# A pinned issue order, a channel mixer in two coupled streams, loads in order of use, and work moved to POOL, in an attention and mixer kernel

## Chip, cores, metric

One core of one Trainium2 chip. The metric is the device time of one execution in microseconds (us); the median of several runs is given. Slow runs are left out of all comparisons. PE is the matrix engine, DVE the vector engine, ACT the scalar engine, POOL the general engine that also issues most loads here.

## The reference, cut

Four batches, eight heads of 768 tokens and 64 columns: attention with a block mask, then a mixer over tokens and one over channels with a hidden width of 2048.

```python
def _attn_ref(q, k, v, sampled_blocks):
    scores = scale * np.matmul(q, k.transpose(0, 1, 3, 2))
    mask = ...                       # neighbours, first and last block, 3 sampled blocks per row
    scores = np.where(mask, scores, -1000000000.0)
    attn = softmax(scores)           # written out with max, exp and sum
    return np.matmul(attn, v)

def _moe_ref(x, alpha1, beta1, w_tok, alpha2, beta2, w_ch1, w_ch2, lam):
    a1 = alpha1 * x + beta1
    tok = np.einsum('ts,bsd->btd', w_tok, a1)
    u = x + lam * tok
    a2 = alpha2 * u + beta2
    ch = np.maximum(a2 @ w_ch1, 0.0) @ w_ch2
    return u + lam * ch
```

## The kernel before

The work is cut into 144 units (4 batches x 4 pairs of heads x 9 units of 1024 score columns). A unit is one set of score products (PE), one exponential (ACT) and, two units later, eight value products (PE). After nine units a pair of heads is normalised (DVE) and goes through the token mixer (`pair_mix`). After four pairs a batch can enter the channel mixer, whose products fill PE beside the next batch's attention. Parts, with cuts marked:

```python
    # weights: each in one piece, issued by POOL ahead of or beside the pairs' loads
    nc.gpsimd.dma_start(w1b[:], moe_w_ch1.rearrange("(o p) n -> p o n", p=P))
    ...
    def prepare(b, n):                       # a pair's casts, transposes and copies
        for i, src in enumerate((q2, k2)):
            nc.vector.tensor_copy(out=rel[...], in_=src[...])
        ...                                  # transposes on PE; q and k copied by DVE
        nc.vector.tensor_copy(out=vx[...], in_=v2[...])      # L220, the value copy

    def pair_mix(b, n):
        nc.vector.tensor_tensor(out=a1p[:], in0=x_sb[...], in1=bc(a1_bc, NT), op=ALU.mult)   # L298
        nc.vector.tensor_tensor(out=a1p[:], in0=a1p[:], in1=bc(b1_bc, NT), op=ALU.add)       # L301
        for g in range(2):                   # 18 token products on PE each
            ...
            nc.vector.tensor_tensor(out=sl, in0=sl, in1=tp[:], op=ALU.add)                   # reads PSUM
            nc.vector.tensor_tensor(out=ub[...], in0=sl, in1=bc(a2_bc, 3), op=ALU.mult)
        ...

    def ch_mix(b):                           # first product, then second: one after the other
        for hf in range(2):
            for f in range(16): ...          # 4 products, relu on ACT or DVE
            for m in range(3):  ...          # 16 products into one bank, added to x_sb, stored

    def setup_ch():
        nc.vector.tensor_copy(out=lam_bcb[:], in_=lam_bc[:])
        nc.vector.tensor_copy(out=be2b[:], in_=be2T[:])
        ...
        for g in range(8):                   # lam is folded into the second weight
            nc.vector.tensor_mul(out=w2b[...], in0=w2b[...], in1=lam_bcb[...])               # L407
```

The softmax here doesn't subtract the row's maximum and nothing guards it: scores larger than these inputs give would overflow.

## Time and profile before

Median 393.35 us (392.55 to 393.9). The profiled run spans 389.8 us.

| stretch of the profiled run before | us |
|---|---|
| start to first score product | 16.6 |
| from there to the first mixer product (in it 11.6 in which nothing computes) | 71.9 |
| from there to PE's last product | 297.4 |
| from there to the end | 3.9 |

The table is read from the timeline of PE: a stretch ends where a named product starts. The shares, the table of stretches and the waits behind it are in the prediction below.

### The profile page before, as it was taken

How to read it: one execution, taken by the hardware profiler on the slowest of the kernel's cores; microseconds unless marked ns; L12 is line 12 of the kernel's file. 1: busy time of each engine (PE TensorE's matmuls, PEld its weight loads, DVE VectorE, ACT ScalarE, POOL GpSimd, SP SyncE). 2: the span in 40 equal slices, each digit the busy share in tenths (PEclk: the TensorE clock that was granted, in tenths of full speed). 3: DMA queues.
4: the chain of work that ended last, by engine and by line, in shares of the span. 5: the costliest groups of instructions: out<-in, count | busy, mean ns of one | idle time of the engine just before them, and what ended most of it. 6: DMA issues, size and time to landing. Idle time of an engine off the chain costs nothing.

```text
span 389.8 us, 7791 instructions
## 1 busy us (share of the span) xinstructions
PE 343.3 (88%) x3398; PEld 219.8 (56%) x3398; DVE 210.3 (54%) x412; ACT 190.2 (49%) x209; POOL 35.9 (9%) x53
## 2 busy tenths in 40 slices
PE   0498089999999999999999999999999999699995
PEld 0276067775655656566656656576656665454442
DVE  3674089776564657374744756565537553632331
ACT  1167066786626655375626654566445564130220
POOL 7152012221011010101000000000000000000000
PEclk9999669999999999999999999999999999999999
DMA  8999994442204132323101000100010001000102
GB/s 190 240 211 205 206 158 64 63 62 27 36 29 102 15 42 49 67 49 42 23 29 54 2 2 29 55 2 2 2 54 29 3 0 56 29 0 27 56 0 81
DMA packets 20781, 23.26 MB, mean 60 GB/s; under 512 B 2068, under 2 KB 16524, under 8 KB 20620
## 3 DMA queue, kind: packets, MB, share of 16 engines
q0 software_dynamic: 15248, 14.42, 23.8%
q1 hardware_dynamic: 5192, 7.96, 5.9%
q8 instruction: 26, 0.43, 0.4%
q10 hardware_dynamic: 308, 0.40, 0.3%
q14 instruction: 7, 0.06, 0.0%
HBM read 30.90 MB, written 6.29 MB: 95 GB/s over the span
## 4 chain that ended last, share of the span: by engine, by line
PE 65%; DVE 12%; DMA 9%; ACT 9%; issue 3%; POOL 1%; ACTq 0%; DVEq 0%; POOLq 0%
PE mm L338 20%; PE mm L363 20%; PE sps L236 10%; ACT eT L245 8%; DMA w2b<-in_moe_w_ch_dram 7%; PE mm L310 6%; PE ops L259 5%; DMA v_103<-in_v_dram 2%; PE mm L213 2%; DVE hts L350 2%; DVE x_sb L318 2%; DVE a1p L298 1%; DVE a1p L301 1%; DVE ub L319 1%; ACT hts L346 1%
## 5 line engine op out<-in xcount | busy, mean ns | idle before, releaser
L245 ACT ACTIVATE eT<-sps,expb 128x1024 f16<-128x1024 f32 x144 | 154.2, 1115 | 115.4 <-PE sps L236 114.5
L338 PE MATMUL mm<-uT,w1b 128*128 128x384 bf16 x512 | 97.5, 325 | 2.8 <-DVE uT L326 0.6
L363 PE MATMUL mm<-w2b,hts 128*128 128x512 bf16 x384 | 91.3, 379 | 0.1
L346 ACT ACTIVATE hts<-mm,b1t 128x384 bf16<-128x384 f32 x64 | 37.1, 580 | 67.7 <-PE mm L338 67.4
L338 PEld LDWEIGHTS <-w1b 128*128 128x128 bf16 x512 | 47.8, 97 | 38.6 <-issue 8.6
L259 PEld LDWEIGHTS <-eT 128*128 128x128 f16 x1152 | 57.8, 99 | 19.7 <-issue 0.6
L350 DVE TENSOR_SCALAR hts<-mm,b1t 128x384 bf16<-128x384 f32 x64 | 39.5, 617 | 49.1 <-PE mm L338 48.9
L363 PEld LDWEIGHTS <-hts 128*128 128x128 bf16 x384 | 34.9, 97 | 35.1 <-issue 0.6
L373 DVE TENSOR_TENSOR ot<-x_sb,mm 128x512 f32<-128x512 f32 x24 | 16.5, 686 | 56.3 <-PE mm L363 56.2
L310 PE MATMUL mm<-a1p,wtokT 128*128 128x128 bf16 x576 | 35.4, 219 | 3.2 <-DVE a1p L301 2.9
L310 PEld LDWEIGHTS <-wtokT 128*128 128x128 bf16 x576 | 33.6, 98 | 5.3 <-issue 4.1
L318 DVE TENSOR_TENSOR x_sb<-x_sb,mm 128x384 f32<-128x384 f32 x32 | 17.6, 551 | 23.1 <-PE mm L310 23.1
L236 PE MATMUL sps<-qx_74,kx_78 88*128 88x512 bf16 (+1 forms) x96 | 24.0, 349 | 5.3 <-ACT eT L245 4.2
L236 PE MATMUL sps<-qx_76,kx_80 88*128 88x512 bf16 (+1 forms) x96 | 22.8, 325 | 3.5 <-ACT eT L245 3.5
L236 PE MATMUL sps<-qx_75,kx_79 88*128 88x512 bf16 (+1 forms) x96 | 25.1, 325 | 0.8 <-ACT eT L245 0.8
L236 PE MATMUL sps<-qx_77,kx_81 88*128 88x512 bf16 (+1 forms) x96 | 25.1, 339 | 0.5 <-ACT eT L245 0.5
L259 PE MATMUL ops<-vext_146,eT 128*128 128x65 f16 x432 | 23.9, 195 | 0.0
L325 PE MATMUL mm<-identb,ub 128*128 128x128 bf16 x96 | 10.0, 225 | 12.5 <-DVE x_sb L318 12.1
L213 PE MATMUL mm<-identb,rel 128*128 128x128 bf16 x192 | 17.1, 230 | 4.0 <-DVE qx_74 L184 4.0
L259 PE MATMUL ops<-vext_147,eT 128*128 128x65 f16 x360 | 20.5, 196 | 0.0
L259 PE MATMUL ops<-vext_148,eT 128*128 128x65 f16 x360 | 19.8, 193 | 0.0
L213 PEld LDWEIGHTS <-rel 128*128 128x128 bf16 x192 | 14.2, 103 | 8.6 <-issue 5.4
(146 smaller groups left out, 239.5 us busy)
## 6 DMA issues: line engine op xcount, KB each, us to landing
out_dram<-ot SPq DMA_DIRECT2D x24, 256.0 KB, 2.0
w1b<-in_moe_w_ch_dram POOLq DMA_DIRECT2D x1, 2048.0 KB, 22.4
w2b<-in_moe_w_ch_dram POOLq DMA_DIRECT2D x1, 2048.0 KB, 26.0
wtk<-in_moe_w_tok_dram POOLq DMA_DIRECT2D x1, 1152.0 KB, 15.0
a_bc<-in_moe_alpha_dram SPq DMA_DIRECT2D x2, 256.0 KB, 11.1
q2f<-in_q_dram SPq DMA_DIRECT2D x1, 384.0 KB, 3.1
k2f<-in_k_dram ACTq DMA_DIRECT2D x1, 384.0 KB, 4.0
lam_bc<-in_moe_lam_dram SPq DMA_DIRECT2D x1, 256.0 KB, 6.7
```

Source lines behind the costliest of these rows:

```text
L213: nc.tensor.transpose(tps[:, o, :], rel[:, a, o, :], identb[:])
L236: nc.tensor.matmul(sps[:, f - u * UN : f - u * UN + w], kx[h][0:KC, ts(jt, P)], qx[h][0:KC, c : c + w], start=True, stop=True,)
L245: nc.scalar.activation(eT[:], sps[:], AF.Exp, bias=expb[:], scale=SCALE)
L259: nc.tensor.matmul(ops[(b, n, a)][:, t, 0 : D + 1], eT[:, ts(i, P)], vx[:, a, jt, 0 : D + 1], start=(r == 0), stop=(jt == NT - 1), skip_gr ...
L310: nc.tensor.matmul(tp[:, j, :], wtokT[:, s, ts(3 * g + j, P)], a1p[:, s, :], start=(s == 0), stop=(s == NT - 1),)
L318: nc.vector.tensor_tensor(out=sl, in0=sl, in1=tp[:], op=ALU.add)
L325: nc.tensor.transpose(up[:, t, :], ub[:, t, :], identb[:])
L338: nc.tensor.matmul(hp[:], w1b[:, dk, ts(f, P)], uT[:, dk, ts(hf, HS)], start=(dk == 0), stop=(dk == 3),)
L346: nc.scalar.activation(hts[:, f, :], hp[:], AF.Relu, bias=b1t[:, f : f + 1], scale=1.0)
L350: nc.vector.tensor_scalar(out=hts[:, f, :], in0=hp[:], scalar1=b1t[:, f : f + 1], scalar2=0.0, op0=ALU.add, op1=ALU.max,)
L363: nc.tensor.matmul(cp[:], hts[:, nk, ts(m, P)], w2b[:, nk, :], start=(nk == 0), stop=(nk == 15),)
L373: nc.vector.tensor_tensor(out=ot[:], in0=x_sb[:, b % NXB * NT + t, :], in1=cp[:], op=ALU.add)
```

## The change

The intent: PE was at 315 us of work in 390, and the rest was to be closed up. The order of instructions on every engine is pinned to the program's, instead of being left to the scheduler. The mask comes first and the first pair is loaded in halves. Loads are issued in the order of use, and the weights in pieces. The channel mixer becomes two streams, so that a group of the first product and a chunk of the second alternate. Scaling the second weight (`w2b`) and the value copies move from DVE to POOL. In batch 0 the token sums come in single tiles. The tail of the last mixer uses the banks that attention has left. The diff, cut to its core:

```diff
+def pin_order(nc, tc):
+    last = {}
+    for ins in list(nc.cur_bb.bb.instructions):
+        prev = last.get(ins.engine)
+        if prev is not None:
+            tc.add_manual_dep(ins, prev, ..., reason="program order")
+        last[ins.engine] = ins.name
...
-        nc.vector.tensor_copy(
+    def put_v(b, n, v2, eng=nc.gpsimd):
+        eng.tensor_copy(out=vx[:, :, :, 0:D], ...)
...
+        m = 1 if b == 0 and n < NPAIR - 1 else 3       # tiles per token group
...
+    def scale_w2(g):
+        if g == 0:
+            nc.gpsimd.tensor_copy(out=lam_bcb[:], in_=lam_bc[:])
+        nc.gpsimd.tensor_tensor(
+            out=w2b[:, 2 * g : 2 * g + 2, :], in0=w2b[:, 2 * g : 2 * g + 2, :],
+            in1=lam_bcb[:].unsqueeze(1).broadcast_to([P, 2, DM]), op=ALU.mult)
...
+    def ch_next(tail=False):
+        ...                                            # what of either product can run
+        if can1 and can2:
+            two = (g2 - 12 * k2) * 16 < f * 12 if k1 == k2 + 1 else True
...
+            if i in (10, 12, 14, 16):                  # w1b in four pieces
+            if i in (20, 22, 24, 26):                  # w2b in four pieces
+            if i == NS:
+                mix_add(None, setup_ch(), i)           # NS = 36: be2b cast, 64 one-column products
+            if NS - 4 <= i < NS + 4:
+                scale_w2(i - NS + 4)                   # units 32 to 39
...
+    while mixq or st["g1"] < NF1 or st["g2"] < NF2:
+        mix_next(i)
+        ch_next(True)                                  # the tail, four banks for the first product
+        i += 1
+    pin_order(nc, tc)
```

## The prediction

> **What bounds the kernel now.** I read the page's busy shares first, then the slices, then busy time by stretches that I cut at the places where the slices change, then the timeline at the cuts. The page:
>
> ```profile
> PE 343.3 (88%) x3398; PEld 219.8 (56%) x3398; DVE 210.3 (54%) x412; ACT 190.2 (49%) x209; POOL 35.9 (9%) x53
> PE   0498089999999999999999999999999999699995
> PEclk9999669999999999999999999999999999999999
> ```
>
> PE is the bound in the middle, but not at the start (first two slices, and a hole at slice 5 with the clock down after it) nor near the end (a dent at slice 35). Busy by stretch:
>
> ```profile
> 0.00:16.60 16.60, 2.27 (x15) 1.41 (x16) 6.86 (x26) 1.28 (x1) 9.02 (x16) 1.00 0.95 216
> 16.60:38.40 21.80, 20.02 (x235) 14.81 (x236) 14.07 (x30) 15.44 (x15) 7.08 (x10) 1.00 1.18 209
> 38.40:50.00 11.60, 0.00 (x0) 0.00 (x0) 1.20 (x3) 0.43 (x1) 1.94 (x3) 0.63 1.25 205
> 50.00:80.00 30.00, 27.89 (x418) 21.69 (x418) 25.93 (x54) 21.75 (x21) 5.72 (x9) 0.91 0.58 84
> 80.00:88.50 8.50, 7.79 (x116) 5.90 (x112) 5.88 (x12) 6.63 (x8) 1.47 (x3) 1.00 0.52 71
> 88.50:334.00 245.50, 238.11 (x2355) 152.01 (x2356) 137.19 (x260) 135.33 (x150) 10.72 (x15) 1.00 0.15 32
> 334.00:341.00 7.00, 3.45 (x45) 2.64 (x45) 5.13 (x9) 0.00 (x0) 0.00 (x0) 1.00 0.11 40
> 341.00:385.90 44.90, 43.80 (x221) 21.38 (x220) 13.43 (x23) 9.30 (x16) 0.00 (x0) 1.00 0.08 30
> 385.90:389.80 3.90, 0.00 (x0) 0.00 (x0) 0.64 (x1) 0.00 (x0) 0.00 (x0) 0.98 0.18 67
> ```
>
> Columns after the length: PE, PEld, DVE, ACT, POOL, clock, DMA share, GB/s. The first score product starts at 16.58; the channel mixer (L338, L363) starts only at 88.5; between 38.4 and 50.0 nothing computes. The timeline names the causes:
>
> ```profile
> 7.02 0.36 DVE L220 COPY vext_146<-v_97 128x768 f16<-128x768 f16 x1 [4.03 <-DMA v_97<-in_v_dram]
> ...
> 13.06 0.36 DVE L220 COPY vext_147<-v_103 128x768 f16<-128x768 f16 x1 [2.24 <-DMA v_103<-in_v_dram]
> ...
> 48.80 0.69 DVE L407 TENSOR_TENSOR w2b<-w2b,lam_bcb 128x1024 bf16<-128x1024 bf16 x1 [11.77 <-DMA w2b<-in_moe_w_ch_dram]
> ...
> 336.65 2.17 PE L310 MATMUL mm<-a1p,wtokT 128*128 128x128 bf16 x36 [2.88 <-DVE a1p L301]
> ```
>
> Three times DVE, which works in order, sat at an instruction whose load had not come while ready work stood behind it (4.0, 2.2 and 11.8 us); at the end PE waits for the last pair's DVE chain with nothing to fill.
>
> "Busy" does not give PE's rate, so I take starts:
>
> ```profile
> 162.74 0.60 PE L236 MATMUL sps<-qx_77,kx_81 88*128 88x256 bf16 x3
> 163.17 0.41 PE L259 MATMUL ops<-vext_147,eT 128*128 128x65 f16 x8
> 163.42 1.02 PE L363 MATMUL mm<-w2b,hts 128*128 128x512 bf16 x4
> 164.28 0.60 PE L236 MATMUL sps<-qx_74,kx_78 88*128 88x512 bf16 x3
> ...
> 189.86 2.17 PE L310 MATMUL mm<-a1p,wtokT 128*128 128x128 bf16 x36
> 191.87 0.81 PE L338 MATMUL mm<-uT,w1b 128*128 128x384 bf16 x4
> 192.52 0.38 PE L236 MATMUL sps<-qx_77,kx_81 88*128 88x512 bf16 x1
> ```
>
> A score unit costs 0.43 us start to start, eight value products 0.24, four second products 0.86, 36 token products 2.01, four first products 0.65; six transposes 0.34 (same stretch). Times the counts: 144 units x 0.67 = 96.5; 16 pairs x (2.01 + 3 x 0.34) = 48.5; first products 128 x 0.65 = 83.2 to 83.5; second 96 x 0.86 = 82.9; weight setup 36 transposes (2.0) and 64 one-column products (1.7). **PE's work is 315 us of the 389.8.** The other 75 us: 16.6 before the first score product; 28.4 up to 88.5 (71.9 long, in which 45 units with their share of the rest need 43.5); 18 in 88.5 to 334 (245.5 for 227.5); 4.7 at the last pair; 3.1 in the last mixer; 3.9 after the last product.
>
> **The Trainium skill.** "Perfetto Trace Analysis", Identifying the Most-Contended Engine: matmul busy share is no measure of headroom, since matmuls are pipelined. The trace agrees: 343.3 busy, 315 of work. "TensorE: Matmul & The Clock Gate", Part 1: after about one idle window (3.4 us) the array falls to half rate, and about as much work brings it back; a 512-column product takes 216 ns at full rate. The trace agrees: clock 0.63 in the hole, eight value products 0.64 us at 50.7 against 0.41 later; 48 second products in 10.37 us. "GPSIMD Engine Reference", 4.1 and 8: two-input elementwise work is about twice as slow there as on DVE, and the engine shares SBUF interfaces with DVE. The kernel before has no such work on POOL, so its trace shows nothing of it.
>
> **The change, part by part.**
>
> *Start.* The mask comes before anything that waits for values, and q and k of the first pair arrive in halves. The table is in by 2.81 (first DVE compare); six compares and maxima and one scale, spaced about 0.2, end near 4.2 instead of 9.2. The full q load took 3.1 us from 1.22, the k load 4.0 from 1.37; halves should be in by 4.5, cast by 5.0. The identity load took 5.0 us from 1.68; it may set the transposes at about 6. Six transposes cold (0.85), a q copy (0.55), the mask copy of 768 columns from PSUM (about 0.9, twice L184's columns): first score product near 8.4. Gain 8.2. The eight warm-up products end near 4.7 and help little.
>
> *Hole.* Scaling w2b (8 x 0.68 us) and the value copies (16 x 0.36) go to POOL; the weights are loaded in pieces at units 10 to 26, after what attention needs. Loads up to unit 36 are some 10 MB, about 50 us at the 205 to 216 GB/s seen, so no faster than wanted, but in order of use. Hole gone: 11.6, and about 2 of cold clock.
>
> *First stage.* I stepped the new loop's counters through by arithmetic (order only, no times). The mixer can't start before batch 0 is mixed: unit 57. Until then a unit's PE work averages 57.5/57 = 1.01 us. ACT needs 1.02 (seven exponentials in 7.14 at 28.70). DVE, per batch 0 pair of nine units: two casts 0.70, four copies 2.2, two normalisations 1.5, a1p 1.9, uT 0.55, and the token sums, now in single tiles, 12 x 0.28 = 3.4 (L318's 0.551 less 256 elements at 0.96 per ns, an estimate): 10.25, or 1.14 a unit. Three engines nearly level, DVE first. I give 17 units at 1.1, 40 at 1.14 and 4 for coupling: **68 us**, 10.5 over PE's work.
>
> *The rest.* From unit 57 on 315 - 57.5 = 257 of PE work. Each unit gets one or two groups of first product and chunks of second, 2.19 us of PE against 1.02 + 0.29 of ACT; the second product has a bank of its own, so an eviction (0.58, 0.62) hides behind it. Of the 7.3% lost in 88.5 to 334 I leave 3%: **265 us**. By the count 44 groups and 45 chunks are left after the last unit, of which some belong to batch 2 and fill the last pair's DVE chain (4.7 gained); with four banks for the first product its 190 ns a piece in the last mixer (1.52 for eight) returns to 163 (3.1 gained).
>
> *End.* Unchanged, 3.9 to 4.1.
>
> Sum: 8.4 + 68 + 265 + 4.1 = 345.5 of span. The median before lies 3.5 above the profiled span; so 349.
>
> **Rivals.**
> 1. *DVE takes the first stage.* With POOL now computing (w2b scaling perhaps 1.4 us each, twice 0.68, by the skill) and sharing with DVE, and one value bank per head from batch 1 on, 1.14 becomes 1.4 a unit, as in 50 to 80 before (21 units in 30 us). For it: DVE 25.93 of 30 there. Against: that stretch held the w2b scaling and cold clock, which go. Time: +12, 361.
> 2. *A fixed order blocks.* If a load is late, or POOL, with value copies behind w2b's wait, is late, everything behind stands, as at 37 to 49 before. For it: POOL issues every later load from the same queue. Against: each load is asked for ten or more units ahead. Time: +5 to +12.
> 3. *The order is better than I grant*: 1% lost after unit 57 and 1.06 a unit before. For it: the interleave leaves no two groups on the same bank within an eviction. Time: 8 + 62 + 260 + 4 = 334, so 338.
> 4. *The gain is given back:* PE-bound anyway, only the start counts. Against: 75 us are not PE work.
>
> **Range and chances.** The fixed parts (315, end 4) are sure to 2; the start to 2; the first stage 62 to 80; the loss after it 1 to 5% (2.6 to 13). Together 340 to 362. Slower or same would need all 40 us of gain lost, with start and hole (20) seen plainly: 0.97 faster, 0.02 same, 0.01 slower.
>
> **What would show it.** First score product at 8 to 9; no DVE wait for w2b and PE clock full from about 10 on; 57 units by 76; DVE over 90% busy in 20 to 70; first L338 near 76 instead of 88.5; PE starts within 3% of work after that; no PE wait for a1p at the last pair; L338 at 163 ns in the last stretch. A hole behind a POOL instruction, or units at 1.4, would make me wrong upwards; DVE well under 90% in the first stage, downwards.

## The result, and the profile after

The changed kernel took 369.48 us (364.88 to 370.0, four runs). The kernel before took 392.95 in the same session (392.08 to 393.9). The ratio is 0.938 (95% interval 0.931 to 0.945). Ratios in this document are the mean time of one kernel's fast runs over that of the other's fast runs of the same rounds, so they are not quite the ratio of the medians. The direction was right, the size was not: 23.5 us gained of 44 expected, 7.5 us above the top of the range.

The profiled run is the fastest of the four (364.88 us, span 363.1). The others span 367 to 368, and what follows is read from the fast one alone.

The page of the changed kernel, busy shares and slices (compare the page of before in the prediction):

```profile
PE 329.7 (91%) x3372; PEld 216.6 (60%) x3406; DVE 219.3 (60%) x413; ACT 191.9 (53%) x212; POOL 77.5 (21%) x95
...
DVE  4479999579856756484666557474646553233221
...
POOL 6876599812300202030300000000000000000000
PEclk9699995599999999999999999999999999999999
```

POOL's busy time has doubled from 35.9 us. The clock is down in slice 2, near the start, and in slices 7 and 8, which is 54 to 73 us, where before it was down in slices 5 and 6. There is still a hole. Busy time by stretches, cut at unit 0, the hole's two ends, the first mixer product and PE's last product (length, then PE, PEld, DVE, ACT, POOL, clock, DMA share, GB/s):

```profile
8.70:51.10 42.40, 39.30 (x554) 30.02 (x554) 34.36 (x79) 38.36 (x38) 31.26 (x42) 0.92 1.15 206
51.10:68.80 17.70, 1.62 (x29) 1.12 (x25) 16.12 (x8) 1.10 (x2) 17.68 (x14) 0.58 0.63 93
68.80:96.50 27.70, 25.29 (x416) 20.60 (x414) 21.87 (x52) 20.59 (x20) 6.67 (x9) 0.96 0.44 61
96.50:359.50 263.00, 257.97 (x2370) 162.76 (x2400) 142.12 (x260) 129.15 (x151) 16.49 (x22) 1.00 0.15 35
359.50:363.10 3.60, 0.00 (x0) 0.00 (x0) 0.62 (x1) 0.00 (x0) 0.00 (x0) 1.00 0.19 73
```

In the hole PE worked for 1.62 of 17.7 us. DVE was "busy" for 16.12 us there with eight instructions, so they averaged 2 us each; those eight are the ones to look at. The timeline of DVE in the hole, where the numbers are start and duration:

```profile
51.13 1.89 DVE L359 TENSOR_TENSOR ub<-x_sb,a_bc 128x128 bf16<-128x128 f32 x1
52.95 0.18 DVE L311 RECIPROCAL rcp<-cp 128x6 f32<-128x6 f32 x1
53.16 0.56 DVE L314 TENSOR_TENSOR x_sb<-cp,rcp 128x384 f32<-128x384 f32 x1
53.64 2.17 DVE L336 TENSOR_TENSOR a1p<-x_sb,a_bc 128x768 bf16<-128x768 f32 x1
55.85 11.23 DVE L339 TENSOR_TENSOR a1p<-a1p,b_bc 128x768 bf16<-128x768 bf16 x1
67.00 0.16 DVE L445 CAST be2b<-be2T 128x4 bf16<-128x4 f32 x1
```

The same addition (L339) took 0.957 us in nearly every other pair. Here it took 11.23. POOL at the same time:

```profile
46.41 8.59 POOL L463 TENSOR_TENSOR w2b<-w2b,lam_bcb 128x1024 bf16<-128x1024 bf16 x4 [0.68 <-DMA w2b<-in_moe_w_ch_dram]
...
57.16 6.26 POOL L463 TENSOR_TENSOR w2b<-w2b,lam_bcb 128x1024 bf16<-128x1024 bf16 x3
63.37 0.81 POOL L261 COPY vext_77<-v_552 128x768 f16<-128x768 f16 x1
64.16 2.11 POOL L463 TENSOR_TENSOR w2b<-w2b,lam_bcb 128x1024 bf16<-128x1024 bf16 x1
```

The last multiplication ends at 66.27 (64.16 + 2.11), and the held addition ends at 67.08, which is 0.81 later: about its own normal duration. The shorter holds fit as well. The row of four from 46.41 ends its third multiplication at 52.85 (three quarters of 8.59), and `ub` ends at 53.02; the fourth ends at 55.00, and the first `a1p` instruction ends at 55.81. The two instructions between, L311 and L314, read PSUM and took their normal 0.18 and 0.56 beside the same multiplications. And PE waited for the cast that stood behind the held addition, in its own timeline:

```profile
67.31 0.56 PE L450 MATMUL mm<-be2b,w1b 128*128 128x1 bf16 x16 [16.08 <-DVE be2b L445]
```

With order pinned, all that PE had to do for the next units stood behind these 16 small products.

The rest of the changed kernel went as predicted: the first score product at 8.03 (predicted 8.4, before 16.58); 263.0 us from the first mixer product to PE's last product (predicted 265); 3.6 to the end (predicted 4.1). At the last pair PE waits 1.39 us for DVE where it waited 2.88:

```profile
290.67 1.17 PE L349 MATMUL mm<-a1p,wtokT 128*128 128x128 bf16 x18 [1.39 <-DVE a1p L339]
```

| stretch | predicted | after, profiled run |
|---|---|---|
| start to first score product | 8.4 | 8.03 |
| from there to the first mixer product, at unit 57 | 68 | 88.4 |
| from there to PE's last product | 265 | 263.0 |
| to the end | 4.1 | 3.6 |
| span | 345.5 | 363.1 |

So the miss lies in one row of the sum. Within it, units 0 to 37, counted from the start of one exponential to that of the other, took 42.4 us, 1.146 each (predicted 1.14); then came the hole; then units 38 to 57 took 27.7 us, 1.46 each (predicted 1.14 too).

### The profile page after: what moved, and what is told of

Read it like the earlier page. It is cut to its first block, busy times and chain, and to the rows that moved or that the text cites. A ratio compares the mean times of both kernels' runs of the same rounds, so it can differ in the third digit from the quotient of the medians.

```text
span 363.1 us, 7834 instructions
## 1 busy us (share of the span) xinstructions
PE 329.7 (91%) x3372; PEld 216.6 (60%) x3406; DVE 219.3 (60%) x413; ACT 191.9 (53%) x212; POOL 77.5 (21%) x95
## 4 chain that ended last, share of the span: by engine, by line
PE 74%; DVE 15%; DMA 5%; POOL 2%; issue 2%; SPq 0%; ACT 0%; ACTq 0%
PE cp L416 18%; PE mm L384 18%; PE sps L276 12%; PE mm L349 8%; PE ops L297 7%; DVE a1p L339 4%; PE ops L416 4%; PE sps L384 4%; PE mm L218 2%; DMA v_165<-in_v_dram 2%; DVE a1p L336 2%; DMA q_339<-in_q_dram 2%; DVE x_sb L314 2%; PE mm L365 1%; DVE ub L359 1%
## 5 line engine op out<-in xcount | busy, mean ns | idle before, releaser
L384 PE MATMUL mm<-uT,w1b 128*128 128x384 bf16 x424 | 85.1, 325 | 0.9 <-ACT hts L392 0.9
L416 PE MATMUL cp<-w2b,hts 128*128 128x512 bf16 x288 | 76.3, 379 | 2.0
L396 DVE TENSOR_SCALAR hts<-mm,b1t 128x384 bf16<-128x384 f32 x42 | 25.9, 616 | 43.1 <-PE mm L384 43.0
L358 DVE TENSOR_TENSOR x_sb<-x_sb,mm 128x384 f32<-128x384 f32 (+1 forms) x44 | 19.5, 443 | 18.8 <-PE mm L349 18.1
L396 DVE TENSOR_SCALAR hts<-sps,b1t 128x384 bf16<-128x384 f32 x22 | 13.6, 617 | 28.2 <-PE sps L384 28.2
L339 DVE TENSOR_TENSOR a1p<-a1p,b_bc 128x768 bf16<-128x768 bf16 x16 | 25.6, 1600 | 0.6
L276 PE MATMUL sps<-qx_67,kx_71 88*128 88x512 bf16 (+1 forms) x96 | 24.4, 355 | 1.4 <-DVE qx_67 L234 1.0
L425 DVE TENSOR_TENSOR ot<-x_sb,cp 128x512 f32<-128x512 f32 x20 | 13.7, 686 | 18.4 <-PE cp L416 18.3
L276 PE MATMUL sps<-qx_68,kx_72 88*128 88x512 bf16 (+1 forms) x96 | 22.9, 333 | 0.0
L359 DVE TENSOR_TENSOR ub<-x_sb,a_bc 128x384 bf16<-128x384 f32 (+1 forms) x44 | 21.9, 498 | 1.5
L276 PE MATMUL sps<-qx_70,kx_74 88*128 88x512 bf16 (+1 forms) x96 | 22.1, 325 | 0.1
L276 PE MATMUL sps<-qx_69,kx_73 88*128 88x512 bf16 (+1 forms) x96 | 22.2, 325 | 0.0
L297 PE MATMUL ops<-vext_75,eT 128*128 128x65 f16 x360 | 19.0, 197 | 0.6 <-DVE x_sb L314 0.6
## 6 DMA issues: line engine op xcount, KB each, us to landing
w1b<-in_moe_w_ch_dram POOLq DMA_DIRECT2D x4, 512.0 KB, 10.1
```

What stands on the lines that cost most here:

```text
L276: nc.tensor.matmul(sps[:, f - u * UN : f - u * UN + w], kx[h][0:KC, ts(jt, P)], qx[h][0:KC, c : c + w], start=True, stop=True,)
L297: nc.tensor.matmul(ops[(b, n, a)][:, t * VW : t * VW + D + 1], eTs[(b, n, u)][:, ts(c, P)], vx[:, a, jt, 0 : D + 1], start=(r == 0), stop= ...
L359: nc.vector.tensor_tensor(out=ub[:, gs, :], in0=sl, in1=bc(a2_bc, m), op=ALU.mult)
L384: nc.tensor.matmul(hp[:, 0:HS], w1b[:, dk, ts(f, P)], uTs[b][:, dk, ts(hf, HS)], start=(dk == 0), stop=(dk == 3),)
L396: nc.vector.tensor_scalar(out=hts[k][:, f, :], in0=hp[:, 0:HS], scalar1=b1t[:, f : f + 1], scalar2=0.0, op0=ALU.add, op1=ALU.max,)
L416: nc.tensor.matmul(cps[k][:], hts[k][:, nk, ts(m, P)], w2b[:, nk, :], start=(nk == 0), stop=(nk == 15),)
```

## The experiments

The first theory: POOL's multiplications of `w2b` hold DVE instructions, and the pinned order hands the hold on to PE. The rivals: w2b's load or product is late; pinning itself blocks; DVE is simply full. In all that follows, "changed" is the changed kernel at 369.48. The medians of the kernel before lay between 391.74 and 392.95 over the sessions of these runs, and each ratio is to that kernel on the same chip.

### Taking the multiplications away from POOL

**e1_no_scale.** Nothing is scaled; the result is wrong.

```diff
-            if NS - 4 <= i < NS + 4:
-                scale_w2(i - NS + 4)
```

> The changed kernel without the eight multiplications of w2b on POOL (wrong result on purpose). Theory A: while POOL runs them (46.4 to 66.2 us), DVE instructions with two SBUF inputs cannot finish (one a1p add took 11.23 us instead of 0.96), and PE starves for 16.6 us. Then the hole and the cold clock after it go: span 363 - 16.6 - 2 = 344 to 347, median 346 to 350, no DVE a1p or ub over 1.2 us. Rival B: a load or a value copy behind the fixed order of POOL is what is late, the long add only shows it; then part of the hole stays with another wait ahead of it, span over 353. Rival C: the first stage is DVE-bound by volume: units 38 to 57 stay at 1.4 us or more, span about 350.

Measured: 353.27 us (352.31 to 355.63), ratio 0.902. The hole shrinks to one PE wait of 3.35 us for the `be2b` cast. About 16 of the 20 us missed hang on eight POOL multiplications and one cast of `lam`. No `a1p` or `ub` took more than 0.96, as theory A said, but its time was missed by 3 us: units 38 to 57 still took 1.46 each and the span is 350.9, which is what rival C had said. So the hole is the multiplications' doing, and the slow units after it are not.

**e2_dve_same.** The same work at the same places, on DVE.

```diff
-            nc.gpsimd.tensor_copy(out=lam_bcb[:], in_=lam_bc[:])
-        nc.gpsimd.tensor_tensor(
+            nc.vector.tensor_copy(out=lam_bcb[:], in_=lam_bc[:])
+        nc.vector.tensor_tensor(
```

> The same eight multiplications at the same places of the order, on DVE instead of POOL. Theory A: no hole of 16 us; DVE gets 8 x 0.68 = 5.4 us more in a stage where it is nearly full, and may wait up to 4 us in order for the w2b pieces (they landed at 46.4 to about 53.7 in the changed kernel, the multiplications stand at units 32 to 39, 44 to 52 us): span 350 to 356, median 352 to 359. Rival B: nothing gained, span 360 or more, since the late load is still waited for. Rival C: volume on DVE is the bound, so moving more to it costs at least 5 us over the run without the multiplications and the units after 38 stay slow.

Measured: 358.79 us (358.29 to 360.83), ratio 0.916. Moving the multiplications back to the engine that was thought too full for them gains 10.7 us. They took 0.68 us each on DVE, and 2.12 on POOL in the changed kernel: the change saved 5.5 us of DVE time here and lost some 16 for it (e1). Rival B is out: at these places DVE did not wait for w2b's load at all, and POOL had waited 0.68 us for it in the changed kernel. One wait of PE remains, 5.62 us before the small products of `be2b` (see e7).

**e3_dve_late.** On DVE, at units 57 to 64, just before the second product needs the weight.

```diff
-            if NS - 4 <= i < NS + 4:
-                scale_w2(i - NS + 4)
+            if 57 <= i < 65:
+                scale_w2(i - 57)
```

> The multiplications on DVE at units 57 to 64, where PE is the bound and DVE has slack, just before w2b is first used (unit 66). Theory A: within 3 us of the run without them, span 345 to 350, median 347 to 352, right result, the best version so far. Rival C: the first stage is as slow as in that run. If DVE is late there after all, evictions of the first product wait for it and it costs up to 5 us more.

Measured: 353.9 us as the median of the fast runs, ratio 0.902. One run of 358.45, the profiled one, counted as slow and is left out. After unit 57 DVE has room, so the multiplications cost next to nothing there: the time is that of the run without them (353.27). The range of theory A (347 to 352) was missed by 2 us.

**e4_pool_spread.** On POOL, but spread: one multiplication for every third unit, from unit 40 to 61.

```diff
-            if NS - 4 <= i < NS + 4:
-                scale_w2(i - NS + 4)
+            if 40 <= i < 64 and i % 3 == 1:
+                scale_w2((i - 40) // 3)
```

> The multiplications stay on POOL but one in every third unit from 40 to 61 instead of eight in a row from 32 to 39. Theory A: each holds a two-input DVE instruction for at most its own 2.1 us, and not every one meets such an instruction, so the hole breaks into pieces: 8 x up to 2.1, half of them met, 6 to 12 us instead of 16.6; span 351 to 360. If the holding is by the row of them without a gap, less: 347 to 352. Rival B (lateness, not sharing): no long DVE instruction and no hole at all, as in the run without them.

Measured: 370.65 us (370.55 to 370.72), ratio 0.945. Spreading them in the program did not help, and all the times expected were missed. POOL still ran them close together (59.00 to 66.04 without a gap), and this time the held instruction is tiny, a cast of four columns with one input, in the timeline of DVE of this run:

```profile
57.59 8.49 DVE L445 CAST be2b<-be2T 128x4 bf16<-128x4 f32 x1
```

It normally takes 0.16 us, and it ends at 66.08 as POOL's row does. So a hold isn't a slower rate, since four columns can't take 8 us at any rate that is merely shared.

### Order, kind of POOL work, and what is left of the first stage

**e5_unpinned.** The changed kernel without its pinned order.

```diff
-    pin_order(nc, tc)
```

> The changed kernel without its pinning of the order: everything else as in the change, but the framework may again order the instructions of an engine by its own model. If the pinning carries the gain of the change, this run is 5 to 20 us slower than the changed kernel (375 to 390); if it only fixes what the written order would give anyway, it is within 3 us (366 to 373); if the fixed order is what makes DVE and PE stand behind the held addition (rival B in its second form: the fault is the order, sharing only starts it), it is faster, 355 to 363.

Measured: 364.79 us (364.0 to 365.07), ratio 0.929. Unpinned, the changed kernel is 4.7 us faster by the medians, but this is not clear of the noise: the intervals of the two ratios overlap (0.926 to 0.932 here, 0.931 to 0.945 there), and the changed kernel's fastest run took 364.88. What differs is where the time goes. The first score product comes at 13.86 instead of 8.03, but the longest PE wait in the hole is 7.52 us instead of 16.08. DVE shows four holds of 1.89 to 2.40 us and one of 8.12, in DVE's timeline and PE's:

```profile
60.30 8.12 DVE L359 TENSOR_TENSOR ub<-x_sb,a_bc 128x128 bf16<-128x128 f32 x1
```

```profile
69.04 0.82 PE L349 MATMUL mm<-a1p,wtokT 128*128 128x128 bf16 x6 [7.52 <-DVE kx L256]
```

The holds are thus not made by pinning; pinning decides how much stands behind them.

**e6_pool_copy.** Each POOL multiplication becomes four copies of one input, in place (no scaling, so a wrong result).

```diff
-        nc.gpsimd.tensor_tensor(out=w2b[...], in0=w2b[...], in1=lam_bcb[...], op=ALU.mult)
+        for h in (2 * g, 2 * g + 1, 2 * g, 2 * g + 1):
+            nc.gpsimd.tensor_copy(out=w2b[:, h, :], in_=w2b[:, h, :])
```

> POOL does four one-input copies of 512 elements at each of the eight places instead of one two-input multiplication of 1024 (wrong result on purpose; about the same POOL time, 2 to 2.5 us a place, if a copy of 512 takes 0.5 to 0.6). If any work of POOL in SBUF holds two-input DVE instructions, the hole of 16 us stays (span 360 to 370, a DVE a1p of over 5 us). If only POOL work with two inputs does, no hole: as the run without the multiplications, span 349 to 354.

Measured: 362.65 us (361.7 to 363.32), ratio 0.924. The first row of sixteen copies stretched `a1p` only to 1.16 and 1.25 us. The second row held `ub`, normally 0.28 us, for 6.14 us:

```profile
63.27 6.14 DVE L359 TENSOR_TENSOR ub<-x_sb,a_bc 128x128 bf16<-128x128 f32 x1
```

So it doesn't take two inputs on POOL's side, and cutting POOL's work in pieces of 0.6 us softens the short holds but doesn't prevent a long one.

**e7_be2b.** As e3, and the `be2b` cast is moved from unit 37 to the end of the token weight's setup.

```diff
     def setup_tok(): ...
+        nc.vector.tensor_copy(out=be2b[:], in_=be2T[:])
     def setup_ch():
-        nc.vector.tensor_copy(out=be2b[:], in_=be2T[:])
```

> The multiplications on DVE at units 57 to 64, and the cast of be2b, which PE's first bias products wait for, moved from unit 37, where it stood behind the normalisation and the 1.9 us of a1p on DVE, to the end of the token setup. In the run with late multiplications PE stood 3.4 to 3.6 us there and the clock fell after it. If that wait is the fixed order's doing, 3 to 6 us come back: median 348 to 351 against 353.9. If DVE's volume is the bound (rival C), the wait moves to the next DVE result and at most 1 us comes back.

Measured: 350.48 us (348.86 to 351.39), ratio 0.892. The PE wait for `be2b` is gone (3.35 us in e1, 3.58 in the profiled run of e3, which was the slow one), and 3.4 us of the time with it. That was a wait that the pinned order had made: a four-column cast behind a normalisation and two `a1p` instructions.

**e8_be2b_m3.** As e7, with token sums in groups of three tiles in batch 0 too, as before.

```diff
-        m = 1 if b == 0 and n < NPAIR - 1 else 3
+        m = 3
```

> As the run before it, and batch 0's token sums in tiles of three again: three pairs with 4 x 0.55 instead of 12 x 0.285 us on DVE, 3.6 us less DVE work in the first stage. If DVE's volume bounds the first stage (rival C), another 2 to 4 us: median 345 to 348. If it is latencies between PE and DVE that bound it, larger tiles cost 0 to 3 us instead: 349 to 353.

Measured: 358.14 us (356.81 to 360.11), ratio 0.913. This is slower by 7.7 us although it saves DVE instructions. But it also changes the plan of the loop: pairs finish sooner in program order, the mixer starts at unit 49 instead of 57, and PE waits up to 2.0 us for a normalised pair. It doesn't tell what DVE's volume is worth; that the smaller tiles, with the plan they bring, are the better choice is as much as it shows.

**e9_less_dve.** As e7, with the `a1p` addition left out for batch 0. This isn't the reference's arithmetic, though the addend is so small that the comparison still passed.

```diff
-        nc.vector.tensor_tensor(out=a1p[:], in0=a1p[:], in1=bc(b1_bc, NT), op=ALU.add)
+        if b > 0:
+            nc.vector.tensor_tensor(out=a1p[:], in0=a1p[:], in1=bc(b1_bc, NT), op=ALU.add)
```

> Base: the version with late multiplications on DVE and the early cast (350.5). Here batch 0's four pairs leave out the second a1p instruction, the addition (not the reference's result, on purpose): 4 x 0.96 = 3.8 us less DVE work before the mixer starts, nothing else moved. In the base unit 57 begins 72 us after unit 0, or 1.265 a unit, against the 1.14 that I had from DVE's volume. If DVE bounds the first stage (rival C), 3 to 5 us come back: 345 to 348. If it is latencies between engines, 0 to 1.5: 349 to 351.

Measured: 346.73 us (346.28 to 346.81), ratio 0.884. Four additions of 0.957 us fewer, 3.8 us of DVE time, made it 3.75 us faster: in this stage this DVE work lay on the path in full. It doesn't tell DVE's volume from a chain, though: in e7 PE stood 1.54 us at 70.72 for an `a1p`, and in e9 this wait is missing.

**e10_putv_dve.** As e7, with the value copies back on DVE, so that POOL computes nothing once the kernel has started up.

```diff
-    def put_v(b, n, v2, eng=nc.gpsimd):
+    def put_v(b, n, v2, eng=nc.vector):
```

> On the base: the value copies back on DVE (0.36 us each, 15 of them, 6 before unit 57) as in the kernel before; POOL then does nothing but issue loads once the loop runs. In the traces so far one or two DVE copies of rel or an addition took 1.2 to 2.3 us beside a POOL value copy or load issue. If sharing with the copies costs DVE more than their own 0.36, this is 1 to 3 us faster (347 to 349); if DVE's volume counts more, 2 us slower (352 to 353).

Measured: 349.71 us (349.37 to 349.81), ratio 0.892. No DVE instruction is held any more (e7 had two of 1.2 to 1.5 us beside value copies). DVE does about 0.36 us more per pair, and the two cancel: against e7 there is no difference beyond the noise. Taking the value copies off DVE was worth nothing.

### Two parts of the prediction measured by themselves

**e11_serial.** As e7, but where both products of the channel mixer could run, the second is always taken first.

```diff
-            two = (g2 - 12 * k2) * 16 < f * 12 if k1 == k2 + 1 else True
+            two = True
```

> On the base: the second product runs as soon as its half of the first is done, all twelve chunks before the next first-product group, so that the two streams no longer alternate (the change's coupling undone, its order otherwise kept). If the alternation is what hides the evictions (my 3 % instead of 7.3 % after unit 57, 11 us), this is 5 to 11 us slower: 355 to 361. If attention between the pieces hides them anyway, within 2 us.

Measured: 359.05 us (358.89 to 360.22), ratio 0.917. Against e7, which ran in the session before, the alternation of the two products is worth 8.6 us.

**e12_no_tail_banks.** As e7, with the tail kept to the banks that the mixer has elsewhere.

```diff
-        ch_next(True)
+        ch_next()
```

> On the base: after the last attention unit the two products get no extra banks (first product on two, second on one). The prediction put 3.1 us on the four banks. If the alternation already hides the eviction of the first product, only the second product's bank is waited for, 0.69 + about 0.2 less the 0.65 of a first-product group, twelve times: 0 to 3 us slower; without any hiding, 3 to 6 us.

Measured: 353.52 us (353.08 to 353.65), ratio 0.901. Against e7 the banks are worth 3.0 us; the prediction's working had 3.1. The runs of e7 spread over 2.5 us, so that this agrees to a tenth is luck. And 3.0 lies on the border between the two expectations, so it doesn't tell which of them holds.

### Pinning again, DVE's volume again, half a dose

These three are built on e10 and ran on one chip.

**e13_unpinned2.** e10 without `pin_order`.

> Base: the version that ran at 349.71 (no POOL multiplication in the first stage, be2b cast early, value copies on DVE); here the order isn't pinned. Theory: pinning was worth nothing in the changed kernel only because the pinned order let a held DVE stop everything behind it; without held instructions the pinned order earns its start (first score product at 8.0 against about 13.9), so this run takes 353 to 356. Rival: the pinned order is worth nothing at all, as 364.8 against 369.5 suggested: 348 to 350.

Measured: 354.3 us (353.01 to 355.45), ratio 0.902. With nothing to hold DVE, the pinned order is worth 4.6 us, as the theory above said. It earns them at the start, as the timelines of this run's DVE and PE show:

```profile
6.43 0.36 DVE L261 COPY vext<-v 128x768 f16<-128x768 f16 x1 [3.44 <-DMA v<-in_v_dram]
6.82 0.68 DVE L192 TENSOR_TENSOR tab<-tab,eqt 24x24 f32<-24x24 f32 x1
```

```profile
11.60 0.49 PE L227 MATMUL sps<-kx,mbb 24*24 24x384 bf16 x1 [6.80 <-DVE mbb L193]
```

The scheduler put a value copy, whose load was still under way, in the middle of the mask's short chain. The first score product comes at 14.53, as against 8.06 in e10. Of these 6.5 us half came back later, although the old hole returned too: the scheduler moved the multiplications of `w2b` ahead of other work again, and DVE and PE stood, in their timelines:

```profile
48.23 0.69 DVE L463 TENSOR_TENSOR w2b<-w2b,lam_bcb 128x1024 bf16<-128x1024 bf16 x1 [6.54 <-DMA w2b<-in_moe_w_ch_dram]
```

```profile
49.36 0.80 PE L349 MATMUL mm<-a1p,wtokT 128*128 128x128 bf16 x6 [4.92 <-DVE x_sb L358]
```

From there on the unpinned run was the faster one: first mixer product to PE's last product took 260.3 us, as against 263.9 in e10. So it is the start that the pinned order earns, and not the rest.

**e14_kx_act.** e10, with the first head's key copy on ACT for the first six pairs: right result, about 3.3 us off DVE.

```diff
-            nc.vector.tensor_copy(out=kx[h][0:D, :], in_=flat[D:P, :])
+            if a == 0 and b * NPAIR + n <= 6:
+                nc.scalar.copy(out=kx[h][0:D, :], in_=flat[D:P, :])
+            else:
+                nc.vector.tensor_copy(out=kx[h][0:D, :], in_=flat[D:P, :])
```

> Same base, with the first head's key copy of the first six pairs on ACT, which takes about 6 x 0.56 = 3.3 us off DVE and gives the right result. Theory (DVE's volume sets the first 57 units, 72.1 us instead of 68): 346 to 347.5, and the first mixer product about 3 us earlier. Rival (ACT's exp chain is as tight as DVE there, so the copies only move the wait): 349 to 351.

Measured: 349.41 us (348.81 to 349.45), ratio 0.890. This is the rival's outcome: 0.3 us, which is within the noise. The first mixer product came at 80.1 instead of 80.5. ACT's busy time between 20 and 40 us rose from 18.34 to 19.44 of 20. So DVE isn't the only bound there: what is taken off it must not go to ACT.

**e15_half_pool.** e10, with the first four multiplications on POOL at units 32 to 35.

```diff
-        nc.vector.tensor_tensor(
+        (nc.gpsimd if g < 4 else nc.vector).tensor_tensor(
...
+            if 32 <= i < 36:
+                scale_w2(i - 32)
-            if 57 <= i < 65:
+            if 61 <= i < 65:
                 scale_w2(i - 57)
```

> Same base, with the first four multiplications of the weight on POOL in units 32 to 35 and the last four on DVE late. Theory A (DVE instructions that touch only SBUF are stretched by a share of POOL's time, half the work for half the loss): 355 to 360. Theory B (one instruction is held until POOL pauses, and the hold hurts only where it falls on an instruction that the exps wait for): either 350 to 353, with the hold hidden behind the queue of scores, or a single hold of about 8 us and 356 to 358, visible as one DVE instruction.

Measured: 354.47 us (353.63 to 354.96), ratio 0.903. Four multiplications cost 4.8 us. That isn't half of the 20, in which other things are too, but about half of the 10.1 that eight cost in e17 below. Neither theory was met in its numbers: there is no single hold of 8 us, but four short ones, of which three follow, with the next addition as a control. POOL's row ran from 47.66 to 56.16, so its multiplications end at 49.78, 51.91, 54.03 and 56.16:

```profile
48.57 1.36 DVE L359 TENSOR_TENSOR ub<-x_sb,a_bc 128x128 bf16<-128x128 f32 x1
...
52.29 1.90 DVE L359 TENSOR_TENSOR ub<-x_sb,a_bc 128x128 bf16<-128x128 f32 x1
...
54.80 2.18 DVE L336 TENSOR_TENSOR a1p<-x_sb,a_bc 128x768 bf16<-128x768 f32 x1
57.02 0.96 DVE L339 TENSOR_TENSOR a1p<-a1p,b_bc 128x768 bf16<-128x768 bf16 x1
```

They end at 49.93, 54.19 and 56.98, that is 0.15, 0.16 and 0.82 us after a multiplication. The addition at 57.02 ran at its normal 0.96 while POOL only issued loads. What the four holds took beyond the normal 0.29 and 0.95 adds up to 4.4 us (1.07, 0.45, 1.61 and 1.23), close to the 4.8 lost.

### What about POOL's work does it

**e16_pool_memset** and **e17_pool_spare**, both on e10, on one chip. At the eight places of the changed kernel, POOL writes a spare tile that nobody reads: by filling it three times, or by multiplying w2b with itself. Results are right, and nothing waits for the tile.

```diff
+    def pool_work(g):                        # e16
+        for _ in range(3):
+            nc.gpsimd.memset(spare[:], 0.0)
+    def pool_work(g):                        # e17
+        nc.gpsimd.tensor_tensor(out=spare[:], in0=w2b[:, 2 * g : 2 * g + 2, :],
+                                in1=w2b[:, 2 * g : 2 * g + 2, :], op=ALU.mult)
...
+            if NS - 4 <= i < NS + 4:
+                pool_work(i - NS + 4)
```

> Base: the version at 349.71. At the eight places where the changed kernel multiplied on POOL, POOL now fills a spare tile with zeros three times (it writes SBUF and reads nothing); the result stays right, nothing waits for the tile. Theory, from the Trainium skill's page SBUF - State Buffer, Who interferes with whom: a DVE instruction with two SBUF inputs contends with a POOL instruction that reads SBUF, not with one that only writes it. So the a1p and ub instructions keep 0.96 and 0.28 us beside the fills, and the time is 349.5 to 351. Rival: any computing on POOL shuts them out, whatever it reads: holds of 1 to 2 us beside the fills, one of over 5, and 355 to 366.

> The counterpart on the same chip: at the same places POOL multiplies w2b by itself into the spare tile, the same size as in the changed kernel, but nothing in the kernel uses the result, which stays right. Theory (POOL's reading alone shuts DVE out; that w2b was late or that something waited for POOL's product plays no part): one hold of over 5 us and several of about 2, all on DVE instructions without a PSUM operand, each ending within 0.9 us after a POOL multiplication ends; 360 to 368. Rival (the dependence on w2b's product or the value copies on POOL made the hole): 350 to 353.

Measured: fills 355.54 us (354.73 to 356.7), ratio 0.906; multiplications 359.82 us (359.27 to 361.88), ratio 0.917. Beside the fills, which kept POOL busy for 24.7 us (12.33 and 12.37), the timeline of DVE shows:

```profile
55.36 0.95 DVE L336 TENSOR_TENSOR a1p<-x_sb,a_bc 128x768 bf16<-128x768 f32 x1
...
59.54 1.18 DVE L261 COPY vext<-v 128x768 f16<-128x768 f16 x1
```

The `a1p` product at 55.36 ran at its normal 0.95 beside fills that lasted until 56.24, and all `ub` instructions beside fills took 0.29. Copies from SBUF to SBUF, normally 0.35, took up to 1.19, and those beside fills ended 0.2 us after one. Seven copies took 5.3 us more than normal, and the run lost 5.8. Beside the multiplications both kinds are held:

```profile
55.00 4.03 DVE L339 TENSOR_TENSOR a1p<-a1p,b_bc 128x768 bf16<-128x768 bf16 x1
...
60.92 2.05 DVE L246 COPY rel<-k 128x768 bf16<-128x768 bf16 x1
```

The theory of e16 was right for the instructions it named and wrong in its time by 4.5 us, because it overlooked the copies. That of e17 missed its longest hold (4.03 us, expected over 5) and its time by 0.2 us, but its cause is confirmed: multiplications that nothing depends on cost 10.1 us (what its eight holds took beyond normal adds up to 11.1). The rival that something waited for w2b's product is out. That w2b's load was late was not removed here, since POOL still reads w2b; e2 rules it out.

## Why the prediction was wrong

The step that failed is the one under "Hole": "Scaling w2b (8 x 0.68 us) and the value copies (16 x 0.36) go to POOL", and from it "Hole gone: 11.6, and about 2 of cold clock". The old hole did go: nothing waits for w2b's load any more. But the work that was moved off DVE came back as holds on DVE. The term that it made wrong is the first stage: 68 us predicted, 88.4 in the profiled run.

By parts:

- **Start**: right (8.4 against 8.03), and e13 shows that the pinned order brings most of it (14.53 without). The sign "PE clock full from about 10 on" failed: from 12 to 16 us the granted clock was 0.50 in the profiled run. In e10 such a difference didn't show in the time: two runs with a mean clock of 1.0 took 349.67 and 349.37, two with 0.985 took 349.81 and 349.76.
- **Rate before the hole**: right (1.14 against 1.146 a unit). Its estimate for the single-tile sums, 0.28, was met too: L358 with 128 columns takes 0.28, and in the trace of before 128 columns more cost 0.135 us (0.686 for the 512 of L373 against 0.551 for the 384 of L318), so that 256 fewer leave 0.28.
- **Hole**: wrong. The prediction said none; in the profiled run it is 16.1 us of PE wait. Deleting the scaling (e1), moving it (e2, e3), and putting foreign multiplications in its place (e17) show its cause. The sign "DVE over 90% busy in 20 to 70" couldn't warn of it: DVE was busy for 44.47 of these 50 us, 89%, but 13.1 of them are what three held instructions took beyond their normal time. Of the 20 us between prediction and median, e2 gives back 10.7 and e3 another 4.9 by choosing a later place; e7 gives 3.4 by taking a small cast out of the queue that the pinned order had made.
- **The rest of the first stage**: with all holds gone (e10) it takes 72.4 us, from 8.06 to 80.48, so 4.4 more than the 68. The sum is nearly right, but its one rate for the whole stage is not: in e10 units 0 to 37 took 1.12 each and units 38 to 57 1.52, and the 4 us given for coupling hid part of that. Up to unit 37 "three engines nearly level" was right (from 20 to 40 us DVE was busy for 18.36 of 20, ACT for 18.34, PE for 17.87), and "DVE first" isn't shown: e9 has DVE's additions on the path, and e14 says that ACT is about as full. From unit 38 to 57 PE was the busiest (25.79 of 28.93 us, DVE 24.02, ACT 20.49). Why these units are slow without any hold wasn't tested.
- **After unit 57**: right (265 against 263.0). The prediction's ground for it, that with two coupled streams an eviction hides behind the other stream, is worth 8.6 us (e11). The tail's banks give 3.0 where 3.1 was worked out (e12). "No PE wait for a1p at the last pair" was wrong: 1.39 us of 2.88 remain.
- **Rivals**: rival 1 named the right pair of engines and the right direction, and was given +12 us. But it expected a rate (1.4 us for a multiplication and 1.4 a unit throughout). It was 2.12 a multiplication, and the units before the hole ran at the predicted rate, since the loss to POOL is a few instructions that stand still. Its 1.4 a unit did come in units 38 to 57 (1.46), but there without POOL's multiplications as well (1.46 in e1, 1.52 in e10). Rival 2, that a fixed order blocks, holds in a second-hand way: the order passes on what POOL does (the longest PE wait is 7.52 us in e5 and 16.08 in the changed kernel, though their times are not clearly apart), and without POOL's work it gains 4.6 us (e13).

The prediction had cited "GPSIMD Engine Reference" for "the engine shares SBUF interfaces with DVE" and read "shares" as a split rate. The Trainium skill says more on another page, which the prediction doesn't cite: "SBUF — State Buffer", Who interferes with whom, calls the shared pair of ports an exclusive lock, which a DVE instruction with two SBUF inputs contends for with a POOL instruction that reads SBUF, and DVE's copies and casts in two-port modes with any POOL instruction. The runs agree: every held instruction here is of one of these two kinds (`a1p` and `ub`; `rel`, the value copy and `be2b`), those that read PSUM were not held in any of these traces, and fills held copies (1.18 us) but not `a1p` (0.95). Had that page been read, the estimate could have been a few `a1p` and `ub` instructions, each waiting for one multiplication, and so something like the 4.8 us of e15; still not the 11.23.

**What stays open.** Why a hold sometimes outlasts several POOL instructions. Short holds end with the POOL instruction beside which they began, or with the first computing one after it; the four long ones (11.23, 8.49, 8.12 and 6.14 us) ended only with the last of a row. In all four of these the row contained one of POOL's value copies among the rest, and in e15 and e17, where POOL makes no such copies, no hold exceeded 4.03. That is a coincidence of six runs and was not tested. Nor is it explained how some holds begin: the 11.23, the 8.49 and the 4.03 began while POOL was only issuing loads. In the changed kernel it issued loads from 54.95 to 57.14; the addition began at 55.85 and would normally have been over at 56.81, before the next multiplication started. The addition of e15 at 57.02 stood beside such loads too and was not held. Also open: why units 38 to 57 are slow without any hold, and what makes the other runs of the changed kernel 5 us longer than the profiled one.

The fastest right versions are e10 and e14 (349.71 and 349.41, ratios 0.892 and 0.890), about 20 us better than the changed kernel: the change, with the scaling on DVE at units 57 to 64, the `be2b` cast early, and, in both, no computing on POOL beside attention.

## What to carry to other kernels

Before moving work from DVE to POOL, list the DVE instructions that will run beside it: two SBUF inputs, or an SBUF copy, means that they may wait for POOL's whole instruction or a row of them. Where DVE was nearly full, the time lost was about the sum of the holds (e15, e16, e17); a later stretch in which DVE has room was the better place for the work (e3). Where the order is pinned, ask of each short instruction that PE waits for what stands ahead of it in its engine's queue, since a fixed order turns one held instruction into a stop of everything. In a trace, compare the duration of one instruction with that of the same instruction elsewhere: a busy engine with few instructions may be a held one.

## What the Trainium skill lacked or had wrong

- "SBUF — State Buffer", Who interferes with whom: the one that issues first has the shared pair "for the whole instruction", and the other blocks. Here it could block for far longer: a DVE addition of 0.96 us took 11.23 beside four POOL multiplications of about 2.1 us and a copy, and a four-column cast took 8.49. The page gives no case of a block over several instructions.
- "GPSIMD Engine Reference", 8: it names the contention and the two kinds of DVE instruction that meet it, without saying that it is a lock, or what it costs. Eight multiplications cost 10.1 us where nothing depended on them (e17 against e10).
- "GPSIMD Engine Reference", 4.1: two-input work is about twice as slow and one-input work roughly at line rate. Measured for 16-bit tiles: a 128x1024 multiplication 2.12 us against 0.68 on DVE (3.1 times), a 128x768 copy 0.82 against 0.36 (2.3 times).
- No page gives POOL's rate for a fill: 128x1024 in 16 bits took 1.03 us (12 in 12.33).
